# One exponential and eight masked copies per tile, with a shorter hardware loop, in a decode-attention kernel

## The chip, the cores and the metric

The kernel runs on one core of a Trainium2 chip. The metric is the device time of one execution in microseconds (us). The median of several executions is what the change is judged by.

## The reference

The reference is attention with one query position per head, over a full cache of keys and values, without a mask:

```python
B, H, Sq, Skv, Dh = 8, 32, 1, 4096, 128        # q, k, v in bf16
scale = q.shape[-1] ** -0.5
scores = jnp.einsum('bhqd,bhkd->bhqk', q, k) * scale
attn = softmax(scores, axis=-1)
return jnp.einsum('bhqk,bhkd->bhqd', attn, v)
```

There are 256 heads. K and V are 256 MB each, and each of their bytes is used once.

## The kernel before

**Tiling.** Eight heads (`G = 8`) make one tile, so there are `NT = 32` tiles. A head's 4096 positions are cut over 16 partitions, 256 positions (`C`) on each; eight heads fill the 128 partitions. A tile of K or of V is 128 x 256 x 128 bf16 and 8 MB. K and V tiles share one pool of three buffers, `kv_pool` (`SLOTS = 3`), which they take in the order k0, k1, v0, k2, v1, k3, v2 and so on. By that order k(t+1) takes the buffer that v(t-2) had, and v(t) takes the buffer of k(t). All of these loads are issued on SyncE's queue (SP), most as one transfer of 8 MB; the first K tile, the last three K tiles and the last V tile come in pieces (`cuts`).

**Scores.** For a tile, `q_prep` spreads the eight query rows over the 128 partitions: a matmul, a copy by ScalarE (ACT), a second matmul and a second copy. `product` lets VectorE (DVE) multiply K by the spread query in place (L185) and fold the 128 products of a position to 64 (L188), and in half of the units of most tiles to 32 (L193). `sum_over_d` lets TensorE (PE) add further with an identity matrix, eight or four matmuls for a unit of 64 positions (L205); `scores_of` reduces the remaining eight columns on DVE (L217). A tile has four such units.

**Softmax.** `weights_of` finds on DVE a maximum for each 32 partitions (L229 to L236) and adds to its negative a table `own`, which is zero for a partition's own head and -1e30 for the seven others; that is `bias` (L240). ACT then computes eight exponentials of the whole score tile, one for each head as a masked column (L249). The masked weights `w` let one matmul serve all eight heads. Each exponential also accumulates its row sum (`esum`).

**Values.** For tiles 0 to 28 `values_loop` multiplies V by the weights in a hardware loop on PE: two matmuls ahead, ten passes of a loop body of `LOOP = 6` matmuls, and two behind. The body's addresses come from registers that PE's sequencer updates, and a branch closes each pass:

```python
with pe.While(lambda: pe.snap(rw, min_val=EDGE * nw, max_val=end) < end):
    ...
    for i in range(LOOP):
        pe.matmul(av, lhsT=wf[:, bass.ds(ow + i * nw, nw)], rhs=vf[:, bass.ds(ov + i * nv, nv)], ...)
    pe.reg_add(rw, rw, LOOP * nw)
    pe.reg_add(rv, rv, LOOP * nv)
```

Tiles 29 to 31 use straight code instead (`values_of`, L316), four column groups of the array side by side. `copy_of` moves the sums to SBUF (`comb`, L344), `result_of` adds up the groups with four matmuls (L360), `norm_of` and `recip_of` make the reciprocal of the row sums, `finish_of` scales two tiles' results at a time (L369), and `store_of` writes them from ACT's queue. Of the last tile the last four rows of V (`LAST = 4`) do not go through `values_of` and `comb`: four matmuls (L354) with a small table of weights, `w_last`, add them straight to the result.

**Order.** The order on PE, DVE, ACT and SP is written by hand in the loop over `t`. In a tile with the hardware loop (`loop`, tiles 1 to 29) the four units of K are multiplied and reduced first; after the fourth `sum_over_d` PE runs `values_loop(t - 1)`, and only behind that SP issues the loads of k(t+1) and v(t). PE works in order, so the `sum_over_d` of tile t+1 stands behind the loop of v(t-1). K(t+1) needs the end of the loop over v(t-2); v(t) needs the last read of k(t), which is the fourth `sum_over_d` of tile t. Tiles 0, 30 and 31 are not `loop` tiles: their loads stand at the head of the iteration.

Of the kernel before, what the change touches and what calls it, by code (L numbers as in the profile page):

```python
# [7 lines left out]
ACT = mybir.ActivationFunctionType  # L8
ALU = mybir.AluOpType
AX = mybir.AxisListType  # L10
BF16 = mybir.dt.bfloat16
F32 = mybir.dt.float32

G = 8
SLOTS = 3
TG = 4
R = 2
OB = 4
LAST = 4
LOOP = 6  # L20
EDGE = 2
NEG = -1.0e30

# [2 lines left out]
def kernel(  # L26
# [7 lines left out]
    nc = tc.nc  # L34
    B, H, Sq, D = q.shape
    S = k.shape[2]
    P = nc.NUM_PARTITIONS
    assert Sq == 1 and D == 128
    NH = B * H
    PH = P // G  # L40
    C = S // PH
    NT = NH // G
    scale = float(D) ** -0.5
    UC = 64
    DS = 512 // UC
    NU = C // UC
    MC = UC
    CB = 4
    RG = R * G
    NQ = NT // R  # L50
    TB = 32
    AG = CB * G
    NV = C // CB
    assert (NV - 2 * EDGE) % LOOP == 0
    assert LAST == CB and TG * AG == P and NH % P == 0 and P % G == 0 and TB % PH == 0 and C % CB == 0

    q_n = q.rearrange("b h o d -> (b h o) d").rearrange("(x p) d -> p x d", p=P)
    o_n = out.rearrange("b h o d -> (b h o) d").rearrange("(n u x) d -> n x u d", u=OB, x=RG)
# [2 lines left out]

    kv_pool = ctx.enter_context(tc.tile_pool(name="kv_pool", bufs=SLOTS))
    consts = ctx.enter_context(tc.tile_pool(name="consts", bufs=1))
    q_pool = ctx.enter_context(tc.tile_pool(name="q_pool", bufs=2))
    w_pool = ctx.enter_context(tc.tile_pool(name="w_pool", bufs=2))
    sc_pool = ctx.enter_context(tc.tile_pool(name="sc_pool", bufs=2))
    small = ctx.enter_context(tc.tile_pool(name="small", bufs=2))
    o_pool = ctx.enter_context(tc.tile_pool(name="o_pool", bufs=1))
    ps_s = ctx.enter_context(tc.tile_pool(name="ps_s", bufs=3, space=bass.MemoryType.PSUM))
# [10 lines left out]
        out=ident[:], in_=ident[:], pattern=[[-1, P]], compare_op=ALU.not_equal,  # L80
# [32 lines left out]
    for j in range(TG):  # L113
# [2 lines left out]
            out=part, in_=part, pattern=[[-1, CB], [CB * G, R], [-CB, RG]],  # L116
            compare_op=ALU.not_equal, fill=1.0, base=0, channel_multiplier=1,
        )
    ones = consts.tile([P, 1], F32, name="ones")
    nc.vector.memset(ones[:], 1.0)  # L120

    w_last = consts.tile([P, LAST, RG], BF16, name="w_last")
    nc.gpsimd.memset(w_last[:], 0.0)
# [4 lines left out]
    def behind_loop(made):  # L128
# [11 lines left out]
        ("k", NT - 3): [C // 2] * 2,  # L140
        ("k", NT - 2): [C // 2] * 2,
        ("k", NT - 1): [C // 4, C // 4, C // 2],
        ("v", NT - 1): [C // 2, C // 4, C // 8, C // 16, C // 32, LAST, LAST],
    }

    def load(kind, t):
# [14 lines left out]
    def q_prep(t):  # L161
        x, p0 = divmod(t * G, P)
        qh = ps_q.tile([G, D], F32, name="qh", tag="qp")
        nc.tensor.matmul(  # L164
            qh[:], lhsT=ident[:, p0 : p0 + G], rhs=q_all[:, x, :], start=True, stop=True
        )
        qg = q_pool.tile([G, D], BF16, name="qg", tag="qg")
        nc.scalar.activation(out=qg[:], in_=qh[:], func=ACT.Copy)  # L168
        qp = ps_q.tile([P, D], F32, name="qp", tag="qp")
        nc.tensor.matmul(qp[:], lhsT=heads[:].rearrange("g h x -> g (h x)"), rhs=qg[:], start=True, stop=True)  # L170
        qb = q_pool.tile([P, 1, D], BF16, name="qb", tag="qb")
        nc.scalar.activation(out=qb[:, 0, :], in_=qp[:], func=ACT.Copy)  # L172
        qbs[t] = qb

    def width_of(t, u):


        return D // 4 if u >= NU // 2 and 0 < t < NT - 3 else D // 2

    def product(t, lo, hi):  # L180
        kt = loads["k", t]
        qb = qbs[t]
        for c0 in range(lo, hi, MC):
            part = kt[:, c0 : c0 + MC, :]
            nc.vector.tensor_tensor(  # L185
                out=part, in0=part, in1=qb[:].to_broadcast([P, MC, D]), op=ALU.mult
            )
            nc.vector.tensor_tensor(  # L188
                out=part[:, :, 0 : D // 2], in0=part[:, :, 0 : D // 2],
                in1=part[:, :, D // 2 : D], op=ALU.add,  # L190
            )
            if width_of(t, c0 // UC) < D // 2:
                nc.vector.tensor_tensor(  # L193
                    out=part[:, :, 0 : D // 4], in0=part[:, :, 0 : D // 4],
                    in1=part[:, :, D // 4 : D // 2], op=ALU.add,
                )

    sums = {}

    def sum_over_d(t, u):  # L200
        kt = loads["k", t]
        ps = ps_s.tile([P, UC, DS], F32, name="ps", tag="ps")
        n = width_of(t, u) // DS
        for s in range(n):
            nc.tensor.matmul(  # L205
                ps[:], lhsT=ident[:],
                rhs=kt[:, u * UC : (u + 1) * UC, s * DS : (s + 1) * DS],
                start=(s == 0), stop=(s == n - 1),
            )
        sums[t, u] = ps  # L210
# [3 lines left out]
    def scores_of(t, u):  # L214
        if u == 0:
            scs[t] = sc_pool.tile([P, C], F32, name="sc", tag="sc")
        made = nc.vector.tensor_reduce(  # L217
            out=scs[t][:, u * UC : (u + 1) * UC], in_=sums.pop((t, u))[:], axis=AX.X, op=ALU.add
        )
        if u == NU - 1:  # L220
            behind_loop(made)

    ws = {}
    esums = {}

    def weights_of(t):
        sc = scs.pop(t)
        pmax = small.tile([P, 1], F32, name="pmax", tag="pmax")
        nc.vector.tensor_reduce(out=pmax[:], in_=sc[:], axis=AX.X, op=ALU.max)  # L229
        spread = small.tile([P, TB], F32, name="spread", tag="spread")  # L230
        nc.vector.tensor_scalar(
            out=spread[:], in0=same[:], scalar1=pmax[:, 0:1], scalar2=-scale,
            op0=ALU.add, op1=ALU.mult,
        )
        nmax = small.tile([P, 1], F32, name="nmax", tag="nmax")
        nc.vector.tensor_reduce(  # L236
            out=nmax[:], in_=spread[:], axis=AX.X, op=ALU.min, apply_transpose=True
        )
        bias = small.tile([P, G], F32, name="bias", tag="bias")
        nc.vector.tensor_scalar(  # L240
            out=bias[:], in0=own[:], scalar1=nmax[:, 0:1], scalar2=None, op0=ALU.add
        )
        w = w_pool.tile([P, C // CB, G, CB], BF16, name="w", tag="w")
        if t % R == 0:
            esums[t // R] = small.tile([P, R, G], F32, name="esum", tag="esum")
        esum = esums[t // R]
        sc_g = sc[:].rearrange("p (i m) -> p i m", m=CB)
        for g in range(G):
            nc.scalar.activation(  # L249
                out=w[:, :, g, :], in_=sc_g, func=ACT.Exp, bias=bias[:, g : g + 1], scale=scale,  # L250
                accum_out=esum[:, t % R, g : g + 1],
            )
        ws[t] = w
        if t == NT - 1:
            nc.gpsimd.tensor_copy(
                out=w_last[:, :, RG - G : RG].rearrange("p m g -> p g m"),
                in_=w[:, (C - LAST) // CB, :, :],
            )

    avs = {}  # L260
    pe = nc.tensor
# [63 lines left out]

    def norm_of(n):
        zp = ps_z.tile([RG, 1], F32, name="zp", tag="zp")
        nc.tensor.matmul(
            zp[:], lhsT=esums.pop(n).rearrange("p r g -> p (r g)"), rhs=ones[:],
            start=True, stop=True,  # L330
        )
        zps[n] = zp

    def recip_of(n):
# [49 lines left out]
    E = mybir.EngineType  # L384
    with tc.manual_schedule(engines={E.PE, E.DVE, E.Activation, E.SP}):
        q_prep(0)
        for t in range(NT):
            loop = 0 < t <= LT
            v_last = t >= NT - 2
            n = t // R - 1  # L390
            if not loop:
                if t + 1 < NT:
                    load("k", t + 1)
                load("v", t)
            product(t, 0, Q)
            sum_over_d(t, 0)
            if 0 < t - 1 <= LT:
                if (t - 1) % R == 0:
                    norm_of(n)
                if t > 1:  # L400
                    result_of(t - 2)
            if t + 1 < NT:
                q_prep(t + 1)
            product(t, Q, 2 * Q)
            sum_over_d(t, 1)
            scores_of(t, 0)
            product(t, 2 * Q, 3 * Q)
            sum_over_d(t, 2)
            scores_of(t, 1)
            if t > 2 and t % R == 1:  # L410
                recip_of(n)
            product(t, 3 * Q, C)
            sum_over_d(t, 3)
            scores_of(t, 2)
            if loop:
                values_loop(t - 1)
                load("k", t + 1)
                load("v", t)
            if v_last:
                values_of(t - 1, 0, C)  # L420
            scores_of(t, 3)
            weights_of(t)
            if t > 2 and t % R == 1:
                finish_of(n)
            if t > 0:
                copy_of(t - 1)
                if t > 2 and t % R == 1:
                    store_of(n)
                if not loop:
                    if t % R == 0:  # L430
                        norm_of(n)
                    result_of(t - 1)
        values_of(NT - 1, 0, C // 2)
        norm_of(NQ - 1)
        recip_of(NQ - 1)
        values_of(NT - 1, C // 2, C - LAST)
        copy_of(NT - 1)
        result_of(NT - 1)
        finish_of(NQ - 1)
        store_of(NQ - 1)  # L440
# [30 lines left out]
```

## Time and profile before

| | |
|---|---|
| median of 10 executions | 1253.25 us (1253.03 to 1253.91) |
| the profiled execution's own time | 1253.61 us |
| its span, from first to last instruction | 1251.8 us |
| busy: PE matmul, DVE, ACT | 767.9, 1036.0, 170.6 us |
| bytes read from HBM | 536.94 MB, 429 GB/s over the span |
| time of the load queue's packets, as a share of 16 DMA engines | 99.3% |

The profile is of one execution. A row of its groups names the source line, the engine, the operation, the tiles written and read, the count, the busy time with the mean of one in ns, and the idle time just before with what ended it. The timeline gives a start, a length, the engine and the line; a bracket at the end holds the idle time before the instruction and what ended it. SPq and ACTq are the queues on which transfers are issued.

### The profile page before, as it was taken

The page shows a single profiled execution, that of the slowest core. Times are in us where ns is not written, and L with a number is a line of the kernel's source. Part 1 is how long each engine was busy: PE and PEld are TensorE (multiplying, and loading weights), DVE is VectorE, ACT ScalarE, POOL GpSimd, SP SyncE. Part 2 cuts the span into 40 slices and gives each one's busy share as a digit, 9 for nine tenths or more (in the row PEclk, how much of TensorE's full clock was granted, in tenths as well). Part 3 has the DMA queues.
Part 4 walks back from the last instruction along what each step waited for, and adds up shares of the span by engine and source line. Part 5 has one row for each costly group of instructions (what it writes and reads, how often), then busy time and mean ns, then how long its engine had stood idle before and what let it go on. Part 6 is the DMA issues. An engine that isn't in the chain of part 4 may idle for free. (4 is left out here: it accounts for less than half of the span.)

```text
span 1251.8 us, 11042 instructions
## 1 busy us (share of the span) xinstructions
PE 767.9 (61%) x3075; PEld 286.9 (23%) x3075; DVE 1036.0 (83%) x586; ACT 170.6 (14%) x625; POOL 3.3 (0%) x18
## 2 busy tenths in 40 slices
PE   2465567755577555775557755577655676556856
PEld 0122122221222112222212221122211222212212
DVE  7887988888987889888798888987889888898783
ACT  0111011111011110111101111011110111101111
POOL 0000000000000000000000000000000000000000
PEclk8677788777887777887788877788777887779867
DMA  9999999999999999999999999999999999999997
GB/s 404 436 436 434 436 436 432 436 436 432 436 434 428 434 425 434 436 436 428 432 433 434 436 436 432 431 434 432 429 433 434 433 430 434 430 431 427 429 442 311
DMA packets 11577, 537.33 MB, mean 429 GB/s; under 512 B 1824, under 2 KB 2080, under 8 KB 2336
## 3 DMA queue, kind: packets, MB, share of 16 engines
q1 hardware_dynamic: 11216, 536.94, 99.3%
q8 instruction: 14, 0.23, 0.1%
q10 hardware_dynamic: 336, 0.07, 0.0%
q14 instruction: 11, 0.09, 0.0%
HBM read 536.94 MB, written 0.07 MB: 429 GB/s over the span
## 5 line engine op out<-in xcount | busy, mean ns | idle before, releaser
L185 DVE TENSOR_TENSOR kt<-kt,qb 128x8192 bf16<-128x8192 bf16 x128 | 565.2, 4416 | 127.0 <-DMA kt<-in_k_dram 98.7
L205 PE MATMUL ps<-kt,ident 128*128 128x512 bf16 x800 | 262.8, 479 | 434.7 <-DVE kt L193 368.5
L288 PE MATMUL av<-vt,w 128*32 x1740 | 424.9, 395 | 4.8
L188 DVE TENSOR_TENSOR kt<-kt 128x4096 bf16<-128x4096 bf16 x128 | 293.4, 2292 | 4.4
L288 PEld LDWEIGHTS av<-vt,w 128*32 x1740 | 172.5, 99 | 262.9 <-issue 121.6
L205 PEld LDWEIGHTS <-ident 128*128 128x128 bf16 x800 | 86.2, 112 | 597.8 <-issue 550.3
L249 ACT ACTIVATE w<-sc,bias 128x256 bf16<-128x256 f32 x256 | 126.3, 494 | 667.9 <-DVE bias L240 667.9
L217 DVE TENSOR_REDUCE sc<-ps 128x64 f32<-128x512 f32 x128 | 87.8, 686 | 57.1 <-PE ps L205 57.1
L193 DVE TENSOR_TENSOR kt<-kt 128x2048 bf16<-128x2048 bf16 x56 | 68.6, 1224 | 1.9
L344 ACT ACTIVATE comb<-av 32x512 bf16<-32x512 f32 (+1 forms) x32 | 18.7, 586 | 323.6 <-PEq L278 313.5
L274 PE MATMUL av<-vt,w 128*32 128x512 bf16 x116 | 47.1, 498 | 14.5 <-issue 13.4
L249 ACT ACTIVATION_READ_ACCUMULATOR w<-sc,bias 128x1 f32 x256 | 47.7, 186 | 0.0
L274 PEld LDWEIGHTS av<-vt,w 128*32 128x32 bf16 x116 | 6.9, 100 | 55.1 <-issue 55.1
L168 ACT ACTIVATE qg<-qh 8x128 bf16<-8x128 f32 x32 | 8.5, 266 | 76.4 <-PE qh L164 76.4
L316 PE MATMUL av<-vt,w 128*32 128x512 bf16 x191 | 16.5, 428 | 1.2 <-DMA vt<-in_v_dram 1.2
L360 PE MATMUL op<-comb,pick 32*16 32x128 bf16 (+1 forms) x128 | 12.3, 215 | 6.2 <-ACT comb L344 6.2
L229 DVE TENSOR_REDUCE pmax<-sc 128x1 f32<-128x256 f32 x32 | 13.4, 420 | 1.1
L170 PE MATMUL qp<-qg,heads 8*128 8x128 bf16 x32 | 6.9, 214 | 11.4 <-ACT qg L168 11.4
L164 PE MATMUL qh<-q_all,ident 128*8 128x128 bf16 x32 | 7.2, 224 | 8.3 <-DMA q_all<-in_q_dram 8.3
L172 ACT ACTIVATE qb<-qp 128x128 bf16<-128x128 f32 x32 | 8.9, 277 | 9.7 <-PE qp L170 9.7
L360 PEld LDWEIGHTS <-pick 32*16 32x16 bf16 (+1 forms) x128 | 6.8, 84 | 13.4 <-issue 13.0
L316 PEld LDWEIGHTS <-w 128*32 128x32 bf16 x191 | 6.9, 105 | 10.3 <-issue 6.2
(29 smaller groups left out, 46.8 us busy)
## 6 DMA issues: line engine op xcount, KB each, us to landing
kt<-in_k_dram SPq DMA_DIRECT2D x6, 4096.0 KB, 24.6
kt<-in_k_dram SPq DMA_DIRECT2D x4, 2048.0 KB, 13.9
vt<-in_v_dram SPq DMA_DIRECT2D x1, 4096.0 KB, 36.0
vt<-in_v_dram SPq DMA_DIRECT2D x1, 2048.0 KB, 40.5
vt<-in_v_dram SPq DMA_DIRECT2D x1, 1024.0 KB, 42.5
vt<-in_v_dram SPq DMA_DIRECT2D x1, 512.0 KB, 43.3
vt<-in_v_dram SPq DMA_DIRECT2D x31, 25.6
kt<-in_k_dram SPq DMA_DIRECT2D x28, 28.1
```

What stands on the lines that cost most here:

```text
L185: nc.vector.tensor_tensor(out=part, in0=part, in1=qb[:].to_broadcast([P, MC, D]), op=ALU.mult)
L188: nc.vector.tensor_tensor(out=part[:, :, 0 : D // 2], in0=part[:, :, 0 : D // 2], in1=part[:, :, D // 2 : D], op=ALU.add,)
L193: nc.vector.tensor_tensor(out=part[:, :, 0 : D // 4], in0=part[:, :, 0 : D // 4], in1=part[:, :, D // 4 : D // 2], op=ALU.add,)
L205: nc.tensor.matmul(ps[:], lhsT=ident[:], rhs=kt[:, u * UC : (u + 1) * UC, s * DS : (s + 1) * DS], start=(s == 0), stop=(s == n - 1),)
L217: made = nc.vector.tensor_reduce(out=scs[t][:, u * UC : (u + 1) * UC], in_=sums.pop((t, u))[:], axis=AX.X, op=ALU.add)
L229: nc.vector.tensor_reduce(out=pmax[:], in_=sc[:], axis=AX.X, op=ALU.max)
L249: nc.scalar.activation(out=w[:, :, g, :], in_=sc_g, func=ACT.Exp, bias=bias[:, g : g + 1], scale=scale, accum_out=esum[:, t % R, g : g + 1],)
L274: pe.matmul(av, lhsT=wf[:, i * nw : (i + 1) * nw], rhs=vf[:, i * nv : (i + 1) * nv], **how)
L288: pe.matmul(av, lhsT=wf[:, bass.ds(ow + i * nw, nw)], rhs=vf[:, bass.ds(ov + i * nv, nv)], start=False, stop=False,)
L316: nc.tensor.matmul(avs[t][j * AG : (j + 1) * AG, :], lhsT=w[:, i, :, :], rhs=vt[:, c0 : c0 + CB, :], start=(i < TG), stop=(j not in group[ ...
L344: nc.scalar.activation(out=comb[0:n, :, :], in_=av[0:n, :, :], func=ACT.Copy)
L360: nc.tensor.matmul(ops[n][:], lhsT=pick[0:e, m, r, :], rhs=comb[0:e, m, :], start=(r == 0 and m == 0), stop=(r == R - 1 and m == CB - 1),)
```

## The change

Seven edits come together.

1. `q_prep` runs two tiles ahead (`q_pool` has three buffers instead of two).
2. `LAST` is 8: the last eight rows of V go straight into the result, in the same pieces as before.
3. `weights_of` computes one exponential per tile into `e`, with the shared maximum as its bias; eight copies with a scale of 0 or 1 for each partition (`mine`) make the masked columns of `w`. The add that made `bias` on DVE is gone, and so is `ones`.
4. The row sums are one column per tile; `norm_of` applies the mask with `mine`, in two matmuls instead of one.
5. In `loop` tiles `product` takes the first two units at once. Both of their `sum_over_d` follow the `norm_of`, `result_of` and `q_prep` work on PE, and the first two `scores_of` follow the third `product`.
6. The hardware loop's body has three matmuls instead of six (`LOOP = 3`), and so twenty passes instead of ten.
7. `sc_pool` has one buffer instead of two.

```diff
-LAST = 4
-LOOP = 6
+LAST = 8
+LOOP = 3
...
-    sc_pool = ctx.enter_context(tc.tile_pool(name="sc_pool", bufs=2))
+    sc_pool = ctx.enter_context(tc.tile_pool(name="sc_pool", bufs=1))
...
-        for c0 in range(lo, hi, MC):
-            part = kt[:, c0 : c0 + MC, :]
+        part = kt[:, lo:hi, :]
...
-        bias = small.tile([P, G], F32, name="bias", tag="bias")
-        nc.vector.tensor_scalar(
-            out=bias[:], in0=own[:], scalar1=nmax[:, 0:1], scalar2=None, op0=ALU.add
+        e = o_pool.tile([P, C], BF16, name="e", tag="e")
+        nc.scalar.activation(
+            out=e[:], in_=sc[:], func=ACT.Exp, bias=nmax[:, 0:1], scale=scale,
+            accum_out=esums[t // R][:, t % R : t % R + 1],
         )
...
         for g in range(G):
             nc.scalar.activation(
-                out=w[:, :, g, :], in_=sc_g, func=ACT.Exp, bias=bias[:, g : g + 1], scale=scale,
-                accum_out=esum[:, t % R, g : g + 1],
+                out=w[:, :, g, :], in_=e_g, func=ACT.Copy, scale=mine[:, 0, g : g + 1]
             )
...
+        esum = esums.pop(n)
+        for r in range(R):
+            nc.tensor.matmul(
+                zp[:], lhsT=mine[:, r, :], rhs=esum[:, r : r + 1], start=(r == 0), stop=(r == R - 1)
+            )
...
         q_prep(0)
+        q_prep(1)
...
-            product(t, 0, Q)
-            sum_over_d(t, 0)
+            product(t, 0, 2 * Q if loop else Q)
+            if not loop:
+                sum_over_d(t, 0)
...
-            if t + 1 < NT:
-                q_prep(t + 1)
-            product(t, Q, 2 * Q)
+            if t + 2 < NT:
+                q_prep(t + 2)
+            if loop:
+                sum_over_d(t, 0)
+            else:
+                product(t, Q, 2 * Q)
             sum_over_d(t, 1)
-            scores_of(t, 0)
+            if not loop:
+                scores_of(t, 0)
             product(t, 2 * Q, 3 * Q)
             sum_over_d(t, 2)
+            if loop:
+                scores_of(t, 0)
             scores_of(t, 1)
```

More of the change, by code (lines that the diff above doesn't have):

```diff
@@ L46 @@
     NU = C // UC
-    MC = UC
     CB = 4
@@ L54 @@
     assert (NV - 2 * EDGE) % LOOP == 0
-    assert LAST == CB and TG * AG == P and NH % P == 0 and P % G == 0 and TB % PH == 0 and C % CB == 0
+    assert LAST % CB == 0 and TG * AG == P and NH % P == 0 and P % G == 0 and TB % PH == 0 and C % CB == 0
     q_n = q.rearrange("b h o d -> (b h o) d").rearrange("(x p) d -> p x d", p=P)
@@ L63 @@
     consts = ctx.enter_context(tc.tile_pool(name="consts", bufs=1))
-    q_pool = ctx.enter_context(tc.tile_pool(name="q_pool", bufs=2))
+    q_pool = ctx.enter_context(tc.tile_pool(name="q_pool", bufs=3))
     w_pool = ctx.enter_context(tc.tile_pool(name="w_pool", bufs=2))
-    sc_pool = ctx.enter_context(tc.tile_pool(name="sc_pool", bufs=2))
+    sc_pool = ctx.enter_context(tc.tile_pool(name="sc_pool", bufs=1))
     small = ctx.enter_context(tc.tile_pool(name="small", bufs=2))
@@ L118 @@
         )
-    ones = consts.tile([P, 1], F32, name="ones")
-    nc.vector.memset(ones[:], 1.0)
+    mine = consts.tile([P, R, RG], F32, name="mine")
+    nc.gpsimd.memset(mine[:], 1.0)
+    nc.gpsimd.affine_select(
+        out=mine[:], in_=mine[:], pattern=[[PH * G, R], [-PH, RG]], compare_op=ALU.is_ge,
+        fill=0.0, base=0, channel_multiplier=1,
+    )
+    nc.gpsimd.affine_select(
+        out=mine[:], in_=mine[:], pattern=[[-PH * G, R], [PH, RG]], compare_op=ALU.is_ge,
+        fill=0.0, base=PH - 1, channel_multiplier=-1,
+    )
     w_last = consts.tile([P, LAST, RG], BF16, name="w_last")
@@ L142 @@
         ("k", NT - 1): [C // 4, C // 4, C // 2],
-        ("v", NT - 1): [C // 2, C // 4, C // 8, C // 16, C // 32, LAST, LAST],
+        ("v", NT - 1): [C // 2, C // 4, C // 8, C // 16, C // 32, LAST // 2, LAST // 2],
     }
@@ L182, in product @@
         qb = qbs[t]
-        for c0 in range(lo, hi, MC):
-            part = kt[:, c0 : c0 + MC, :]
+        part = kt[:, lo:hi, :]
+        nc.vector.tensor_tensor(
+            out=part, in0=part, in1=qb[:].to_broadcast([P, hi - lo, D]), op=ALU.mult
+        )
+        nc.vector.tensor_tensor(
+            out=part[:, :, 0 : D // 2], in0=part[:, :, 0 : D // 2],
+            in1=part[:, :, D // 2 : D], op=ALU.add,
+        )
+        if width_of(t, lo // UC) < D // 2:
             nc.vector.tensor_tensor(
-                out=part, in0=part, in1=qb[:].to_broadcast([P, MC, D]), op=ALU.mult
-            )
[L188 to L196, printed above, removed]
+                out=part[:, :, 0 : D // 4], in0=part[:, :, 0 : D // 4],
+                in1=part[:, :, D // 4 : D // 2], op=ALU.add,
+            )
     sums = {}
@@ L238, in weights_of @@
         )
-        bias = small.tile([P, G], F32, name="bias", tag="bias")
-        nc.vector.tensor_scalar(
-            out=bias[:], in0=own[:], scalar1=nmax[:, 0:1], scalar2=None, op0=ALU.add
+        if t % R == 0:
+            esums[t // R] = small.tile([P, R], F32, name="esum", tag="esum")
+        e = o_pool.tile([P, C], BF16, name="e", tag="e")
+        nc.scalar.activation(
+            out=e[:], in_=sc[:], func=ACT.Exp, bias=nmax[:, 0:1], scale=scale,
+            accum_out=esums[t // R][:, t % R : t % R + 1],
         )
         w = w_pool.tile([P, C // CB, G, CB], BF16, name="w", tag="w")
[L244 to L247, printed above, removed]
+        e_g = e[:].rearrange("p (i m) -> p i m", m=CB)
         for g in range(G):
             nc.scalar.activation(
-                out=w[:, :, g, :], in_=sc_g, func=ACT.Exp, bias=bias[:, g : g + 1], scale=scale,
-                accum_out=esum[:, t % R, g : g + 1],
+                out=w[:, :, g, :], in_=e_g, func=ACT.Copy, scale=mine[:, 0, g : g + 1]
             )
@@ L254, in weights_of @@
         if t == NT - 1:
[L255 to L258, printed above, removed]
+            for i in range(LAST // CB):
+                nc.gpsimd.tensor_copy(
+                    out=w_last[:, i * CB : (i + 1) * CB, RG - G : RG].rearrange("p m g -> p g m"),
+                    in_=w[:, (C - LAST) // CB + i, :, :],
+                )
     avs = {}
@@ L327, in norm_of @@
         zp = ps_z.tile([RG, 1], F32, name="zp", tag="zp")
[L328 to L331, printed above, removed]
+        esum = esums.pop(n)
+        for r in range(R):
+            nc.tensor.matmul(
+                zp[:], lhsT=mine[:, r, :], rhs=esum[:, r : r + 1], start=(r == 0), stop=(r == R - 1)
+            )
         zps[n] = zp
```

## The prediction

> **What bounds the kernel now.** I read the page first: busy shares, the load queue, the DVE row.
>
> ```profile
> PE 767.9 (61%) x3075; PEld 286.9 (23%) x3075; DVE 1036.0 (83%) x586; ACT 170.6 (14%) x625; POOL 3.3 (0%) x18
> ...
> q1 hardware_dynamic: 11216, 536.94, 99.3%
> ...
> L185 DVE TENSOR_TENSOR kt<-kt,qb 128x8192 bf16<-128x8192 bf16 x128 | 565.2, 4416 | 127.0 <-DMA kt<-in_k_dram 98.7
> ```
>
> The load queue's packets fill 99.3% of the span: the loads bound it, and DVE waits for K. Next, the timeline of one middle tile (start, length, queue or engine):
>
> ```profile
> 424.88 0.33 SPq L151 DMA_DIRECT2D vt<-in_v_dram  x1
> 426.11 14.81 PE L288 MATMUL av<-vt,w 128*32 x60
> 431.29 4.42 DVE L185 TENSOR_TENSOR kt<-kt,qb 128x8192 bf16<-128x8192 bf16 x1 [4.47 <-DMA kt<-in_k_dram]
> 433.42 0.97 PEld L288 LDWEIGHTS av<-vt,w 128*32 x6 [0.53 <-issue]
> 434.93 0.97 PEld L288 LDWEIGHTS av<-vt,w 128*32 x6 [0.53 <-issue]
> 441.70 0.33 SPq L151 DMA_DIRECT2D kt<-in_k_dram  x1
> ```
>
> DVE sat 4.47 us until K landed. The next such start is at 469.92, so a tile takes 38.7 us, which is two loads of 19.35 us. V is issued at 424.88, the loop runs, and the next K is issued when it ends, 16.8 us later. Loads stay queued: K issued at 480.68 stands behind a V that lands at 489.16. The loop is regular: a pass of six weight loads each 1.51 us, with a hole of 0.53.
>
> Then the timeline of the end:
>
> ```profile
> 1161.60 15.02 PE L288 MATMUL av<-vt,w 128*32 x60
> ...
> 1179.39 0.69 DVE L217 TENSOR_REDUCE sc<-ps 128x64 f32<-128x512 f32 x1 [3.46 <-PE ps L205]
> 1180.00 4.42 DVE L185 TENSOR_TENSOR kt<-kt,qb 128x8192 bf16<-128x8192 bf16 x1
> ...
> 1237.98 0.27 PE L360 MATMUL op<-comb,pick 128*16 128x128 bf16 x2 [2.78 <-ACT comb L344]
> ...
> 1242.38 5.49 PE L316 MATMUL av<-vt,w 128*32 128x512 bf16 x31 [1.25 <-DMA vt<-in_v_dram]
> ```
>
> Here the cover is thin. In tile 30 DVE waits 3.46 us at its first `scores_of`, because the `sum_over_d` in front stands on PE behind the loop over v(28), which ends at 1177.4. From 1179.39 on DVE has no wait for K any more, only for PE's fixed 3.06 us, until the last weights. PE starts on the last V at 1238.0 and finds itself waiting for V at 1242.38, by just 1.25 us. So **the DVE chain of the last two tiles has 1.25 us of slack** to the loads, where a middle tile has 4.47.
>
> [...] matmul starts 0.427 us apart where the granted clock is 0.5, and 0.215 where it is 1.0. [...] the best slices show 436.
>
> **The change, part by part.**
>
> *The loop body of three.* In the trace PE's sequencer, not the array, sets a warm pass: its register operations follow each other by 0.153 us, one for each matmul, and from the last one over the two adds, the branch and the next pass's start it takes 0.586. That is 6 x 0.153 + 0.586 = 1.505, the 1.51 seen; six matmuls alone need 6 x 0.215 = 1.29. With three: 3 x 0.153 + 0.586 = 1.045 us, against 0.753 for half an old pass. A loop that is warm throughout grows by 20 x 1.045 - 10 x 1.505 = **5.85 us**. Cold passes are bound by the array (3 x 0.427 = 1.28), so a loop with six to eight cold matmuls, the usual one, grows by about 5.2.
>
> *In a middle tile* this is covered. Everything behind the loop moves 5.2 us: SP's next K, ACT's `comb` copy, PE's next sums. K: issued at 480.68 + 5.2 = 485.9, while the V in front has its last packet at 488.7, so 2.8 us are left. The first load of the kernel needs 1.0 to 1.8 us from issue to the first packets on all 16 engines; it holds by 1 us. Sums: the new order puts the first two behind the loop and the small PE work, some 5.1 us (1.5 for `norm_of`, `result_of`, `q_prep` with its wait for ACT's copy; 3.6 for 16 warm matmuls). The cycle from the second `scores_of` to the next one is 0.64 + 26.8 (third product's end to K's issue, before) + 5.2 + 5.1 = 37.7 us, below 38.7: no stall, by 1 us. V's issue depends on DVE, and DVE's work in front is 0.3 us shorter (two instructions fewer, some 0.15 fixed each, from 2.292 and 1.224 us for 4096 and 2048 elements).
>
> *At the end* it is not covered. Tile 29: the loop over v(27), behind which K was issued at 1140.41, ends 0.3 earlier by DVE and 5.2 later by its passes, at 1145.3; the second sum ends 5.1 later, `scores_of` takes 0.61 more, and the fourth product starts at 1151.1 instead of 1150.30: **+0.8**. The new order gives back most of the 5.2 here, since three products instead of two stand in front of the wait (3.56 us at 1142.36 now). The loop over v(28) starts 0.8 later, is warm throughout (15.02 us), and grows by 5.85. Tile 30 has the old order, so its first `scores_of` waits for that loop: **+6.65 us** (1179.39 to 1186.0). No later wait takes any of it up: K(31) has landed by 1208.35, before its third product would want it (1213.47 + 6.4). v(30) is issued at 1204.3 instead of 1197.65, still ahead of K(31)'s end.
>
> *One exponential and eight copies.* [...] Gain 0.1, between -0.6 and +0.7. The dropped `bias` add saves 0.27 us of the chain in tile 30 and again in 31. In middle tiles the weights are used a tile later: nothing.
>
> *The rest.* `norm_of`'s second matmul: 0.2 us on PE, in front of matmuls that wait anyway. `q_prep` earlier: its copies are short (0.27) and were never last. One `sc` buffer: the exponential has read it 13 us before DVE writes it again. The eight rows: one `values_of` matmul less, up to 0.1, and `comb` no longer waits for the last but one piece; four more L354 matmuls (0.4) lie beside `comb`'s 0.61. POOL's table and second small copy are off every path. Fewer ACT and DVE instructions mean fewer instruction fetches, and each takes a load engine about a microsecond; this could bring the last V forward by 1 us, but then V no longer sets the end.
>
> **The sum.** PE can start on the last V at 1237.98 + 6.65 - 0.54 - 0.08 = 1244.0. Its 62 matmuls took 3.06 us (1238.04 to 1241.1) and 5.54 (1242.38 to 1247.92). With that mix of clocks the end would be at 1252.6 (+4.7); warm throughout, where the same matmuls need 5.8 us (the 5.6 us that were cold count half), at 1249.8 (+1.9). V has landed, so it is one unbroken run and warms sooner than before: I take **+3.5**. The tail behind it (`comb`, four matmuls, scale, store) is unchanged. Span 1255.3, the execution's own time 1253.61 + 3.5 = 1257.1; the median stands 0.36 below that execution: **1256.8 us**. With 0.7 either way for the chain and 0.6 for the copies, my own range is 1.3 to 6.3 more.
>
> **Rivals.**
>
> *No slower: the loads still end last.* Place: the branch of the loop. If the sequencer runs ahead of the array, a pass of three stays near 0.75 us. With an extension of e for each loop, tile 29 moves by e - 4.4, tile 30 by 1.12e more, and the slack is 1.25 + 0.6; the sides part at e = 2.9, a pass of 0.90 us. Below that the loads decide, and fetches and rows give 0.3 to 1.3: about 1252.3; if the fetches of the slowest load engine all went, 1250.5. For it: the changed order removes DVE's 3.56 us wait of tile 29. Against: the register operations keep their 0.153 step whatever the array does. 0.15 for no measurable difference, 0.04 for faster.
>
> *Much slower: K is issued late in every tile.* If the margins of 1.0 us fail, each further us of loop costs half a us per tile, since K(t+2) hangs on k(t) over two tiles: 14 us for each us, 1262 to 1285. For it: two margins of 1 us. 0.09.
>
> *The clock drops inside the loop.* Three matmuls in 1.045 us keep the array 62% busy, 86% now. Stretches of 26% (before 1238.9) lost the clock; one of 55% (406.1 to 409.5) kept it. If 62% lost it, each loop would grow by a further 4.7 us, the cycle become 42.4, and the time 1253 + 28 x 3.7 = 1357. 0.03.
>
> *The change not doing what it says* has no room here: counts and order are in the code.
>
> **How the numbers follow.** My case has 0.69 and gives 1254.6 to 1259.6. The range 1252.2 to 1262.5 takes in it, most of the first rival and a little of the second, 0.82 in all. A measurement can tell 0.2%, 2.5 us, from no change. Slower by more: 0.62 of my case, the second and third rival, 0.74; my case's lower end and the first rival make 0.22 within; 0.04 faster.
>
> **What would show it.** Right: passes of 1.04 us; the middle tile still 38.7 us, with DVE's wait for K near 5; K issued 5 us later after V; DVE's wait at tile 30's first `scores_of` some 9.6 us (3.46 + 6.65, less the 0.53 by which DVE itself comes later); PE starting on the last V near 1244.0, with no wait for V inside. Wrong: a pass near 0.75, waits for V at the end as before, or DVE's wait for K growing and DMA slices below 425 GB/s.

## The result and the profile after

The changed kernel takes **1279.05 us** (median; 1277.24 to 1283.64) against 1253.22 for the kernel before on the same chip: a ratio of **1.0208** (95% interval 1.0199 to 1.0217), 25.8 us slower. The prediction had said 1256.8, in a range of 1252.2 to 1262.5. The direction was right and the size was not.

The page of the changed kernel, with the lines that answer to those shown of before:

```profile
PE 818.3 (64%) x3110; PEld 288.8 (23%) x3110; DVE 1023.2 (80%) x495; ACT 166.0 (13%) x433; POOL 4.1 (0%) x22
...
q1 hardware_dynamic: 11216, 536.94, 98.4%
...
L192 DVE TENSOR_TENSOR kt<-kt,qb 128x8192 bf16<-128x8192 bf16 (+1 forms) x99 | 560.8, 5665 | 150.9 <-DMA kt<-in_k_dram 144.0
...
L256 ACT ACTIVATE w<-e,mine 128x256 bf16<-128x256 bf16 x256 | 105.6, 494 | 1.1
...
vt<-in_v_dram SPq DMA_DIRECT2D x31, 26.3
kt<-in_k_dram SPq DMA_DIRECT2D x28, 24.0
```

DVE's busy time fell, and the queue's packets still fill 98.4% of a span that grew by 24.7 us (1251.8 to 1276.5). The same bytes take longer while the queue looks full. **A queue whose packets fill the span isn't thereby at full speed**: the share counts the time that packets are under way, and a slow packet counts for more. By the two pages 98.4% went with 421 GB/s here, and 99.3% with 429 before. The last two lines give the count of loads and the median from issue to landing. For K it was 28.1 us before and is 24.0 now. A load needs 19.35 us by itself (half of the 38.7 us of a tile before); the rest is the time for which it stood behind another, and what it loses. Call the time from a load's issue to the landing of the load in front of it its *lead*. For K the median lead was 8.7 us before and is 3.75 now.

The timeline of two middle tiles, in the columns used before:

```profile
430.56 0.33 SPq L159 DMA_DIRECT2D vt<-in_v_dram  x1
437.19 8.69 DVE L192 TENSOR_TENSOR kt<-kt,qb 128x16384 bf16<-128x16384 bf16 x1 [4.96 <-DMA kt<-in_k_dram]
438.83 0.40 PEld L295 LDWEIGHTS av<-vt,w 128*32 x3 [0.65 <-issue]
439.84 0.44 PEld L295 LDWEIGHTS av<-vt,w 128*32 x3 [0.60 <-issue]
...
453.05 0.33 SPq L159 DMA_DIRECT2D kt<-in_k_dram  x1
...
469.38 0.33 SPq L159 DMA_DIRECT2D vt<-in_v_dram  x1
477.59 8.69 DVE L192 TENSOR_TENSOR kt<-kt,qb 128x16384 bf16<-128x16384 bf16 x1 [6.53 <-DMA kt<-in_k_dram]
...
491.83 0.33 SPq L159 DMA_DIRECT2D kt<-in_k_dram  x1
...
493.50 6.25 PE L212 MATMUL ps<-kt,ident 128*128 128x512 bf16 x20
```

A pass now has three weight loads and repeats after 1.01 to 1.05 us. V is issued at 430.56 and K 22.49 us later, where it was 16.8. DVE's starts on K are 40.40 us apart (437.19 to 477.59), where a tile took 38.7; the next one comes 38.88 later, so a long tile is followed here by a short one. DVE's wait for K is *longer* in the long tile, 6.53 against 4.96: DVE isn't late, K is.

The same stretch cut at the landings: K at 437.11, V at 456.47, K at 477.47, V at 496.80. The columns are the length in us, the busy time of PE, PEld, DVE, ACT and POOL, the granted clock, the DMA share and GB/s:

```profile
437.11:456.47 19.36, 15.18 (x66) 5.50 (x65) 19.21 (x4) 1.13 (x3) 0.00 (x0) 1.00 1.04 433
456.47:477.47 21.00, 11.92 (x40) 4.05 (x38) 13.03 (x13) 4.15 (x11) 0.00 (x0) 0.76 0.99 418
477.47:496.80 19.33, 15.18 (x56) 5.42 (x57) 19.14 (x4) 1.13 (x3) 0.00 (x0) 0.92 1.00 434
```

The two V loads take 19.36 and 19.33 us. The K between them, issued at 453.05, 3.42 us before V in front of it landed, takes 21.00 at 418 GB/s, with a DMA share of 0.99. That is where the time goes. Count what each load takes beyond 19.35 us (a piece: its share of that), from the landing in front to its own, as its loss. Summed over all loads the loss is 0.9 us for K and 4.9 for V in the kernel before, and **23.5 for K** and 3.1 for V in the changed one: 20.8 us more together. The last piece of V lands at 1268.45 instead of 1247.36, 21.1 us later. From that landing to the end of the span it is 8.05 us instead of 4.44, another 3.6. The two make 24.7 us, which is all that the span grew.

The timeline of the end:

```profile
1207.04 0.69 DVE L224 TENSOR_REDUCE sc<-ps 128x64 f32<-128x512 f32 x1 [9.47 <-PE ps L212]
...
1264.99 0.27 PE L368 MATMUL op<-comb,pick 128*16 128x128 bf16 x2 [2.94 <-ACT comb L352]
1265.25 3.53 PE L323 MATMUL av<-vt,w 128*32 128x512 bf16 x29
1268.72 3.83 PE L323 MATMUL av<-vt,w 128*32 128x512 bf16 x30
1272.66 0.60 ACT L352 ACTIVATE comb<-av 128x512 bf16<-128x512 f32 x1 [7.72 <-PE av L323]
```

DVE's wait at tile 30's first `scores_of` grew from 3.46 to 9.47 us. PE starts on the last V at 1265.25 and runs through without a wait for V: each piece is there when PE comes to it (the last lands at 1268.45), and the chain of DVE and PE sets the end.

### The profile page after: what moved, and what is told of

It reads as the page before. It is cut to its first block, busy times and chain, and to the rows that moved or that the text cites. A ratio compares the mean times of both kernels' runs of the same rounds, so it can differ in the third digit from the quotient of the medians.

```text
span 1276.5 us, 11990 instructions
## 1 busy us (share of the span) xinstructions
PE 818.3 (64%) x3110; PEld 288.8 (23%) x3110; DVE 1023.2 (80%) x495; ACT 166.0 (13%) x433; POOL 4.1 (0%) x22
## 3 DMA queue, kind: packets, MB, share of 16 engines
q1 hardware_dynamic: 11216, 536.94, 98.4%
## 5 line engine op out<-in xcount | busy, mean ns | idle before, releaser
L192 DVE TENSOR_TENSOR kt<-kt,qb 128x8192 bf16<-128x8192 bf16 (+1 forms) x99 | 560.8, 5665 | 150.9 <-DMA kt<-in_k_dram 144.0
L295 PE MATMUL av<-vt,w 128*32 x1740 | 487.5, 399 | 102.6 <-issue 102.0
L212 PE MATMUL ps<-kt,ident 128*128 128x512 bf16 x800 | 247.9, 471 | 283.1 <-DVE kt L200 230.0
L195 DVE TENSOR_TENSOR kt<-kt 128x4096 bf16<-128x4096 bf16 (+1 forms) x99 | 288.8, 2917 | 3.4
L295 PEld LDWEIGHTS av<-vt,w 128*32 x1740 | 169.6, 97 | 429.2 <-issue 353.2
L256 ACT ACTIVATE w<-e,mine 128x256 bf16<-128x256 bf16 x256 | 105.6, 494 | 1.1
L249 ACT ACTIVATE e<-sc,nmax 128x256 bf16<-128x256 f32 x32 | 16.2, 508 | 567.8 <-DVE nmax L243 567.8
L368 PEld LDWEIGHTS <-pick 32*16 32x16 bf16 (+1 forms) x128 | 8.7, 83 | 28.3 <-issue 27.9
```

The costliest lines, as they stand in the source:

```text
L192: nc.vector.tensor_tensor(out=part, in0=part, in1=qb[:].to_broadcast([P, hi - lo, D]), op=ALU.mult)
L195: nc.vector.tensor_tensor(out=part[:, :, 0 : D // 2], in0=part[:, :, 0 : D // 2], in1=part[:, :, D // 2 : D], op=ALU.add,)
L212: nc.tensor.matmul(ps[:], lhsT=ident[:], rhs=kt[:, u * UC : (u + 1) * UC, s * DS : (s + 1) * DS], start=(s == 0), stop=(s == n - 1),)
L249: nc.scalar.activation(out=e[:], in_=sc[:], func=ACT.Exp, bias=nmax[:, 0:1], scale=scale, accum_out=esums[t // R][:, t % R : t % R + 1],)
L256: nc.scalar.activation(out=w[:, :, g, :], in_=e_g, func=ACT.Copy, scale=mine[:, 0, g : g + 1])
L368: nc.tensor.matmul(ops[n][:], lhsT=pick[0:e, m, r, :], rhs=comb[0:e, m, :], start=(r == 0 and m == 0), stop=(r == R - 1 and m == CB - 1),)
```

## The experiments

My theory by then: the body of three is the whole cost, in two places. K, issued too short a time before the load in front of it lands, loses time in the middle, and the last tiles lose 4 to 5 us more by their chain. The main rivals: the other six edits carry a part of the cost; passes of three cost something on PE other than by their length; the loss lies in K's size or in its shape as one large transfer.

| kernel | median us | ratio to before (95%) |
|---|---|---|
| changed | 1279.05 | 1.0208 (1.0199 to 1.0217) |
| changed, body of 6 | 1252.15 | 0.9990 (0.9981 to 0.9999) |
| changed, body of 4 | 1252.26 | 0.9991 (0.9982 to 1.0000) |
| changed, body of 12 | 1252.80 | 0.9995 (0.9986 to 1.0003) |
| before, body of 3 | 1392.44 | 1.1110 (1.1087 to 1.1132) |
| before, one exponential | 1253.61 | 1.0001 (0.9993 to 1.0010) |
| changed, 3 in the loops over v(27) and v(28), else 6 | 1257.65 | 1.0034 (1.0022 to 1.0047) |
| changed, 6 in these two, else 3 | 1274.53 | 1.0176 (1.0159 to 1.0193) |
| changed, body of 6 and 26 matmuls more | 1273.68 | 1.0159 (1.0142 to 1.0176) |
| changed, K in 1/8 and 7/8 | 1281.04 | 1.0218 (1.0182 to 1.0253) |
| changed, K in 1/4, 1/4, 1/2 | 1270.33 | 1.0142 (1.0125 to 1.0159) |

### The changed kernel with a body of six

```diff
-LOOP = 3
+LOOP = 6
```

> The changed kernel with LOOP = 6 again, all other edits kept. Theory A (the longer loop alone costs, by K loads issued too late and by the DVE chain of the last tiles): the loop takes 16.8 us again, K is issued over 8 us before the V in front lands, and the time is 1252 us (1251 to 1253.3). Theory B (one of the other edits, the joined product, the order or the one exponential, costs): it stays above 1265 us.

It took 1252.15 us, 26.9 less than the changed kernel. One constant gives the whole loss back, so beside a body of six the six other edits cost nothing. The page and the timeline of its end:

```profile
vt<-in_v_dram SPq DMA_DIRECT2D x31, 25.8
kt<-in_k_dram SPq DMA_DIRECT2D x28, 28.4
```

```profile
1175.21 0.69 DVE L224 TENSOR_REDUCE sc<-ps 128x64 f32<-128x512 f32 x1 [2.83 <-PE ps L212]
...
1241.48 5.42 PE L323 MATMUL av<-vt,w 128*32 128x512 bf16 x30 [1.22 <-DMA vt<-in_v_dram]
```

K's 28.4 us, DVE's short wait in tile 30 and PE's wait of 1.22 us for the last V are back, all three nearly as in the kernel before.

### The kernel before with a body of three

```diff
-LOOP = 6
+LOOP = 3
```

> The kernel before with LOOP = 3 alone. Theory A: in the old order DVE's first scores of a tile wait on PE behind the loop, so PE and DVE form one cycle of 35.9 us (first scores to K's issue) + 5.6 (longer loop) + 1.95 (first sum) = 43.5 us a tile against 38.7: 1253 + 27 x 4.8 = about 1383 us. A rival, that lateness of K is all and the order does not matter: about 1279 us, as the changed kernel.

1392.44 us: the shorter body alone costs the *old* order 11%, five times what it costs the new one. Its waits on DVE (us in total, times, longest), and its SP queue:

```profile
DVE sc L217 <- PE ps L205: 310.9, 61, 11.4
...
DVE kt L185 <- DMA kt<-in_k_dram: 7.4, 5, 3.7
```

```profile
445.84 0.33 SPq L151 DMA_DIRECT2D kt<-in_k_dram  x1
...
489.31 0.33 SPq L151 DMA_DIRECT2D kt<-in_k_dram  x1
```

A tile takes 43.5 us (445.84 to 489.31), and DVE hardly waits for K (7.4 us in all) but 310.9 us for PE: in the old order the first `scores_of` stands behind only two products, and every tile has the stall that tile 30 has in the changed kernel. So the body belongs together with the other edits, which make it cost 2% and not 11%; by these waits it is the new order that does so, though the others were not taken out one by one. Here K is issued 0.6 us *after* the V in front has landed, and V with a lead of 0.9 us (medians), and **both** lose: 3.3 us per load of K, of which the empty queue itself is 0.6, and 1.6 per load of V, on average. The loss isn't K's own.

### A body of three in the last two loops alone, and everywhere else

```diff
+        LP = 3 if t >= NT - 5 else 6     # first kernel; LP in place of LOOP
+        LP = 6 if t >= NT - 5 else 3     # second kernel
```

> The changed kernel with LOOP = 6, but 3 for the last two loops (v27 and v28) alone. Theory A: the DVE chain of the last tiles comes 6 to 7 us later, V is covered at the end, and the time is that of LOOP = 6 throughout plus 3.5 us, 1255.5 us (1254.5 to 1257.5). Rival, that the last tiles' chain has cover and all of the loss sits in the middle tiles: within 0.5 us of LOOP = 6 throughout.

> The changed kernel with LOOP = 6 in the last two loops (v27 and v28) alone and 3 in all others: the complement of the run before with 3 in the last two. If the two losses add up, the last tiles' 5.5 us go and the time is 1273.5 us (1272 to 1276). If the last tiles cost nothing beside late loads, it stays at 1279 us.

The first took 1257.65 us, 5.5 above the body of six; the second 1274.53, 22.4 above it. The sum, 27.9, is within a microsecond of the 26.9 of both together, so the losses add. The first shows the end with nothing of the middle; its timeline:

```profile
1188.45 0.69 DVE L224 TENSOR_REDUCE sc<-ps 128x64 f32<-128x512 f32 x1 [9.48 <-PE ps L212]
...
1246.60 3.58 PE L324 MATMUL av<-vt,w 128*32 128x512 bf16 x29
1250.12 3.83 PE L324 MATMUL av<-vt,w 128*32 128x512 bf16 x30
```

DVE's 9.48 us and PE's unbroken last run are those of the changed kernel. Its last V lands at 1249.79, and the tail behind that is 8.11 us. This kernel is what my prediction described, +4.4 us, and it lies within 1 us of the predicted 1256.8, a little above the 1254.5 to 1257.5 expected of it here. That it lies so near is in part luck: the end costs 5.5 us and not 3.5, and the other edits start it from 1252.15, 1.1 us lower than the kernel before. The other 21.4 us that the prediction missed are in the middle.

### A body of four, and one of twelve

```diff
-LOOP = 3
+LOOP = 4     # and, in the other kernel, 12
```

> The changed kernel with LOOP = 4. A pass is 4 x 0.153 + 0.586 = 1.20 us, fifteen of them 18.0 us, so a loop is 2.8 us longer than with 6, half of what LOOP = 3 adds. Theory A with a threshold (K's lead over the V in front falls from 8.6 to about 5.8 us[...]): 1252 to 1253.5 us. Rival, each us of loop costs: half of the loss, about 1265 us.

> The changed kernel with LOOP = 12: five passes, bound by the array (12 x 0.215 = 2.58 us against 12 x 0.153 + 0.586 = 2.42), 12.9 us a loop instead of 15.1. If the loads are the bound again and all leads are wide, this brings nothing over LOOP = 6: 1252.2 us, within 0.5. If shorter loops still help somewhere, 1251 us or less.

The body of four takes 1252.26 us, no more than six. Its page:

```profile
kt<-in_k_dram SPq DMA_DIRECT2D x28, 25.7
```

25.7 less 19.35 leaves K a lead of over 6 us, and its 28 loads lose 0.9 us in all. So the cost has an edge, between leads of 3 to 4 us and of 6. Twelve gives nothing beyond six: once the load is there in time, PE's shorter loop is worth nothing to a kernel that waits for loads (1252.80 us against 1252.15).

### A body of six, with the loop's length put back by other means

```diff
-LOOP = 3
+LOOP = 6
...
+    zero = consts.tile([P, CB * G], BF16, name="zero")
+    nc.gpsimd.memset(zero[:], 0.0)
...
+            for i in range(26):
+                pe.matmul(av, lhsT=zero[:], rhs=vf[:, i * nv : (i + 1) * nv], start=False, stop=False)
```

> The changed kernel with LOOP = 6 and, between the ten passes and the two closing matmuls, 26 more matmuls with zero weights (they add nothing), 26 x 0.215 = 5.6 us: a loop as long as with LOOP = 3, without its twenty branches. Theory A, that only the length of the loop counts: K is issued 22.4 us after V again, and the time is that of the changed kernel, 1279 us (1274 to 1283). Theory C, that the branches or the register operations themselves slow the loads: 1252 to 1258 us, where 1258 is the last tiles' share.

The 26 matmuls stand between the hardware loop and its last two matmuls and add zeros. The timeline of PE:

```profile
439.83 6.62 PE L298 MATMUL av<-vt,w 128*32 x26
446.46 5.78 PE L306 MATMUL av<-vt,zero 128*32 128x512 bf16 x26
...
454.54 3.63 PE L215 MATMUL ps<-kt,ident 128*128 128x512 bf16 x16
```

They take 5.78 us, what the body of three adds. The time rises to 1273.68, 21.5 us of the 26.9. It is just under the band of 1274 to 1283 that I gave. So the *length* in front of K's issue is the cause of most of it, however PE spends that time.

Here PE is dense up to the sums, and 16 matmuls of these take 3.63 us at full clock. In the changed kernel they fall to half clock in eleven of the tiles 5 to 28: 20 in 6.25 us at 493.50 above, where the tile before needed 4.62. In eleven of these 24 tiles DVE then waits for PE at one of the first two `scores_of`, 8.1 us in all; with the 26 matmuls it never does. The longest of these waits, and the first `scores_of` of tile 29, in the changed kernel:

```profile
539.51 0.69 DVE L224 TENSOR_REDUCE sc<-ps 128x64 f32<-128x512 f32 x1 [1.37 <-PE ps L212]
...
1169.86 0.69 DVE L224 TENSOR_REDUCE sc<-ps 128x64 f32<-128x512 f32 x1 [6.43 <-PE ps L212]
```

and that of tile 29 with the 26 matmuls:

```profile
1166.81 0.69 DVE L227 TENSOR_REDUCE sc<-ps 128x64 f32<-128x512 f32 x1 [4.76 <-PE ps L215]
```

Yet tiles 5 to 28 take 39.48 us on average here and 39.49 in the changed kernel. So K's late issue is enough for all that the middle loses. Of the 3.4 us between the two profiled executions 1.7 come at tile 29, where the wait is 4.76 us instead of 6.43; the medians are 5.4 apart, and the rest is not accounted for.

### K in smaller pieces

```diff
-    cuts = {
+    cuts = {("k", t): [C // 8, 7 * C // 8] for t in range(1, NT - 3)}       # first kernel
+    cuts = {("k", t): [C // 4, C // 4, C // 2] for t in range(1, NT - 3)}   # second kernel
+    cuts |= {
```

> The changed kernel (LOOP = 3) with the K loads of tiles 1 to 28 in two transfers, an eighth and seven eighths. DVE still has to wait for the second one. Theory D, that a fresh transfer starts slowly because of its size (8 MB rows of 64 KB): the small first one starts at once and covers the start of the second, K loses under half of its 21 us, 1258 to 1266 us. Theory E, that any K issued late starts slowly whatever its size: 1277 to 1281 us.

> The changed kernel (LOOP = 3) with the K loads of tiles 1 to 28 in three transfers, a quarter, a quarter and a half. DVE may start on the first half 9.7 us before the whole tile is in; its wait for K was 5 to 6.5 us. If the loss is a ring from K's landing over DVE and the loop to the issue of the next but one K, an earlier start of DVE opens the ring: V and K are issued up to 5 us earlier, K has a lead over 6 us again, and the time is 1252 us plus the last tiles' 5.5 or less, 1252 to 1258 us. If the ring is not what sets the time: 1270 us or more.

A first piece of an eighth doesn't help: 1281.04 us. Its DMA issues (count, KB each, median us to landing):

```profile
kt<-in_k_dram SPq DMA_DIRECT2D x28, 7168.0 KB, 23.9
...
kt<-in_k_dram SPq DMA_DIRECT2D x28, 1024.0 KB, 7.3
```

By itself 1 MB takes 2.42 us at the loads' rate. The 16 such pieces that had a lead under 4 us took 3.62 on average (2.44 to 5.43), the ten with more 2.66 (2.45 to 3.28). The seven eighths behind them lost 0.03 us each. So the loss sits at the start of a fresh load and doesn't come from its size.

Three pieces let DVE start on the first quarter, and I expected 1252 to 1258. They gave 1270.33: **a miss**. The waits of DVE and its timeline say what took over:

```profile
DVE sc L225 <- PE ps L213: 207.7, 89, 9.5
```

```profile
453.65 0.69 DVE L225 TENSOR_REDUCE sc<-ps 128x64 f32<-128x512 f32 x1 [4.64 <-PE ps L213]
455.84 0.69 DVE L225 TENSOR_REDUCE sc<-ps 128x64 f32<-128x512 f32 x1 [1.50 <-PE ps L213]
...
468.09 8.69 DVE L193 TENSOR_TENSOR kt<-kt,qb 128x16384 bf16<-128x16384 bf16 x1
...
492.59 0.69 DVE L225 TENSOR_REDUCE sc<-ps 128x64 f32<-128x512 f32 x1 [3.42 <-PE ps L213]
494.25 0.69 DVE L225 TENSOR_REDUCE sc<-ps 128x64 f32<-128x512 f32 x1 [0.97 <-PE ps L213]
```

DVE has no wait for K left (the product at 468.09 starts without one) and 207.7 us of waits for PE. The second `scores_of` is at 415.74, 455.84 and 494.25: 78.51 us for two tiles, 39.26 each. That is the ring of PE and DVE that the prediction put at 37.7 us, "no stall, by 1 us". It is longer than the two loads too, so K's loss hid a second limit of nearly the same size: by this trace the changed kernel would still take more than 38.7 us a tile if its K lost nothing.

### One exponential and eight copies, on the kernel before

```diff
-                out=w[:, :, g, :], in_=sc_g, func=ACT.Exp, bias=bias[:, g : g + 1], scale=scale,
-                accum_out=esum[:, t % R, g : g + 1],
+                out=w[:, :, g, :], in_=e_g, func=ACT.Copy, scale=mine[:, 0, g : g + 1]
```

with `e`, `mine` and the two matmuls of `norm_of` as in the change.

> The kernel before with the one exponential, the eight masked copies and the two norm matmuls alone. Weights of a middle tile are used a tile later and the last tiles' weights have 1.25 us of cover, so nothing changes: 1253.2 us, within 0.5. Rival, that eight copies behind one exponential delay the last tile's weights beyond that cover: 1254.5 us or more.

1253.61 us, ratio 1.0001 (0.9993 to 1.0010): nothing. By itself the edit that the change is named for neither costs nor gains.

## Why the prediction was right or wrong

**The bound** (two loads of 19.35 us a tile): right, until the loads themselves grew longer. The best slice of the page before shows 442 GB/s, not 436; a full load moves 8.39 MB in 19.35 us, 433.5 GB/s.

**The pass of the loop**, 1.045 us: right. Weight loads of a pass start 1.01 to 1.05 us apart in the changed kernel, and V to K went from 16.8 to 22.5 us, 5.7 more, where the forecast had 5.2. The rival that the sequencer would run ahead fell with it.

**K in the middle tile: "it holds by 1 us". This is the step that failed.** The lead was forecast well: 2.8 us to the last packet of V, and 3.42 to its landing in the stretch shown. What was wrong is what a load needs. I took 1.0 to 1.8 us, from an issue to the first packets on all 16 engines, out of the kernel's first load, where nothing was in front: its first packet came 1.02 us after the issue. But the time to the first packet isn't the time to full rate, and that same load showed it: in the records of the kernel before its first 14 packets of 16 KB took 1.0 to 1.4 us each, the later ones 0.61 (median), and its 2 MB landed 7.31 us after the issue, where 19.35 us for 8 MB make 4.84. Loads of K over the changed kernel and the two with the same loss (26 matmuls more; six in the last two loops), sorted by lead, lost:

| lead, us | mean loss, us | least to most | loads |
|---|---|---|---|
| under 2 | 1.87 | 1.4 to 2.2 | 3 |
| 2 to 3 | 1.31 | 0.8 to 2.3 | 5 |
| 3 to 3.5 | 1.27 | 0.0 to 2.6 | 18 |
| 3.5 to 4 | 0.68 | 0.0 to 2.0 | 21 |
| 4 to 4.5 | 0.48 | 0.0 to 1.3 | 15 |
| 4.5 to 5 | 0.31 | 0.0 to 0.7 | 7 |
| 5 and more | 0.0 | -0.2 to 0.0 | 9 |

A lead of about 5 us was needed, not 1.8. In the changed kernel K's packets of 64 KB that start 1.0 to 1.5 us after the issue take 2.95 us on average and up to 3.65; in the kernel before, where K is not yet at its turn then, every packet takes 2.42, and K's own first packets do so too. From 5 us after the issue on it is within 0.05 us of that again.

The lead follows from a sum. From K's landing to V's issue the stretch shown takes 32.3 us (437.11 to 469.38), from there to the issue of the K after next 22.4 (491.83). Two tiles of loads last 77.4 us, so 22.7 are left for that K from issue to landing, and less its own 19.35 its lead would be 3.3 us at full rate. With 16.9 and 19.8 us from V to K the same sum gives 8.9 for a body of six and 6.0 for one of four, and the median leads there were 8.96 and 6.26. At 3.3 us K loses about 1.3. What it loses makes the loads behind it land later, and gives the next K more lead: behind the loss of 1.65 us at a lead of 3.42 the next K has 4.98 and loses 0.19. So the kernel settles where its losses give back the lead that is missing: K's 28 whole loads lose 0 to 2.5 us each, 0.75 on average, and tiles 5 to 28 take 39.49 us on average, where they took 38.80 before. The rival "K is issued late in every tile" was priced at 1262 to 1285, which holds the result; its mechanism is the one that happened, and it had a chance of 0.09.

**The ring of DVE and PE, "37.7 us".** A second term that was too small, by 1.5 us. In the changed kernel, where DVE waits for K in each tile, it shows only now and then, in the waits of eleven tiles, 8.1 us in all; with K in three pieces it shows in full, at 39.26. Two tiles of that trace split it. From the start of the second `scores_of` to the next issue of K I had 0.64 + 26.8 + 5.2 = 32.6 us; it took 33.08 both times (415.74 to 448.82, 455.84 to 488.92), 0.4 more. From there to the next second `scores_of` I had 5.1; it took 7.02 and 5.33, 1.1 more on average. In the changed kernel the same step, K's issue to the end of the first two sums, is 5.30 us or, in eleven of 24 tiles, 6.75 to 6.98, where the sums run at half clock. I had taken 16 warm matmuls for it.

**The end: right in its mechanism, too small by 1 to 2 us.** DVE's wait in tile 30 is 9.47 us, with 9.6 forecast. PE starts on the last V 27.2 us later than before (1238.04 to 1265.25); less the 21.1 of the loads that is 6.1, with 6.0 forecast. The tail behind the last landing grew by 3.6, with 3.5 forecast. PE did warm sooner: the granted clock is 0.78 from 1265.25 to 1272.66, with 7.41 us of PE's work, and was 0.65 from 1238.04 to 1247.92 before, with 8.63. Tile 29 was later than I had it, its fourth product 7.66 us behind the loop's end instead of 5.8. And the experiments put the end at 4.5 us (taken out of the changed kernel) to 5.5 (alone), not 3.5: alone, the last V also lands later, at 1249.79 instead of 1246.47 with a body of six, where I had the loads unchanged.

**One exponential and eight copies: right.** The page above has 494 ns for one copy; the eight of the last tile follow each other by 0.40 us (1260.91 to 1264.12). With the exponential and its sum they take 3.84 us there (1260.28 to 1264.12), where the eight exponentials and their sums took 3.94 (1233.17 to 1237.11): the gain of 0.1 that I forecast by an estimate of my own, with no trace of such a copy. The other edits cost nothing beside a body of six, as forecast. Of the instruction fetches the two pages count 25 packets before and 22 in the changed kernel. In the records of the kernel before those of 16 KB take 0.90 to 1.10 us each, and beside one mostly 15 packets of the load queue are under way instead of 16. That fewer fetches bring the last V forward isn't shown.

**The clock inside the loop: right.** (The stretch from 406.1 to 409.5 that I gave as 55% busy holds 1.74 us of work in 3.40, 51%.) The first of the three stretches holds most of a loop and shows 1.00: passes of three kept the full clock, and the rival that they lose it fell.

## What to carry to other kernels

A load that is "in time" because the one in front is still under way may not be: measure how long before the end of the one in front it must be issued to keep the full rate (here about 5 us), and forecast with that margin, not with the time to the first packet. When two margins of a microsecond hold up a forecast of no loss, give that forecast no more than an even chance, and price what happens when one fails in every tile: here the first 2.9 us of a longer loop (the body of four) were free, and the next 2.8 cost about 21 us over the middle tiles. And look at bytes per second by stretch, not at the queue's busy share, which stayed at 98.4%.

## What the runs showed of the hardware that was not expected

- A load of K issued under some 5 us before the one in front of it lands starts slowly: up to 2.6 us lost per 8 MB; V does so too where its lead is under 2 us (1.7 us, in the old order with a body of three). A small first piece doesn't mend it. Not every such load loses: at the end of the changed kernel V(30), with a lead of 3.16 us, lost under 0.1. Why the first packets are slow, and what else beside the lead decides it (the work of DVE and PE at that time was not varied), isn't shown by these runs and stays open.
- The granted clock fell to half at 493.74, behind a stretch of 3.41 us (490.33 to 493.74) in which PE was busy for 2.00 us, 59%. In the kernel before a stretch of 51% (406.1 to 409.5) had kept it. So the busy share of a stretch alone doesn't tell whether it loses the clock.
